# Sliding-window attention and a SwiGLU block: the tail tile of batches 2 and 3 in its own turn, attention paced closer, and most of block 5 moved to seven products

## The chip, the cores and the metric

The kernel runs on one core of a Trainium2 chip. The metric is device time of one execution in microseconds (us). Before the change the median of three runs is 332.56 us (332.44 to 333.28). One further execution was recorded by the hardware profiler; it took 333.68 us, and its first and last instruction are 331.9 us apart.

Engines are named as the profile names them: PE (matrix products; PEld is its weight load), DVE (vector), ACT (scalar), POOL (here only a queue that issues the loads) and SP (a queue that issues transposing DMAs and the stores).

## What is computed

The reference, cut to what matters (8 batches, 8 heads, 576 tokens, 64 values per head; 4608 tokens of 512 values; 1536 hidden columns):

```python
scores = q @ k.T / 8 - slope[h] * |i - j|          # only for 0 <= i - j < 128
x = (softmax(scores) @ v)                           # (4608, 512)
g, val = x @ w_gate, x @ w_val                      # (4608, 1536) each
out = (g * sigmoid(g) * val) @ w_out                # (4608, 512)
```

## The kernel before, in words

**Attention.** Two batches make a group `s` of nine tiles of 128 tokens: tiles p = 0 to 3 and 4 to 7 belong to one batch each, and p = 8, the tail tile, holds the last 64 tokens of both. That gives 36 units i = 9s + p, which are worked in order. `scores(i)` (L289) makes the products of a unit's keys with its own and the next tile's queries (`scores_128` or `scores_two` at the edges of a batch), takes the exponential on ACT and multiplies by the mask on DVE; `weighted(i)` (L406) multiplies by the values, and DVE divides by the sum (L431, L432). A group's tail tile needs two more sets of products: `scores_two` (keys of tiles 3 and 7, queries of the tail) and `tails()` (the tail with itself). In group 0 both are made at p = 8. In the later groups `tails()` is made together with the scores of p = 3 and `scores_two` together with those of p = 7.

**Where q and k come from.** POOL's queue loads each rank's q, k and v in order (`load`, `load_qk`, `load_v`); the q and k tiles have five buffers each (L143). From rank 11 on SP's queue transposes them by DMA (`transpose`, L247) into `kT` (12 slots) and `qT` (9 slots). `order` (L232) is the order of the transposes, `need` how many must be done before a unit, `due(rank)` (L241) the unit by which `ahead(i)` (L920) may send one: all that are due by unit i + AHEAD (4) and loaded are sent after unit i. In groups 1 to 3 the tail's q and k are loaded right behind rank 9s + 3 (L905) and transposed right behind the group's fourth tile, five ranks before their turn. The x tile of a unit is transposed by SP too (L451), and the stores share that queue; POOL's and SP's orders are fixed by hand from unit 7 on.

**The feed-forward part.** The 4608 rows of x are nine blocks of 512 tokens; block 8 holds the tails. For blocks 0 to 5 `gate_val(n, m)` makes one of twelve hidden columns of 128 from four products with w_gate and four with w_val, each 512 wide (L488): tanh on ACT and a `scalar_tensor_tensor` on DVE for the gate (L506, L507), a copy on ACT and a product on DVE for the value (L520, L521). Blocks 6 to 8 go by `gate_val_by_seven` (L714): a pair u of hidden columns is made as a 2 by 2 block product with seven instead of eight products, each four matmuls of width 256 (L726). These need sums of the weights, `gate_val_weight_sums(u)` (L696, four DVE instructions), and sums of x, `x_sums(n)` (L705, four), made beforehand. The output product of the block before, `strassen(n, t)` (L608, 2 times 7 parts of six matmuls, L636), is dealt out between these; its sums of h (`sums`, L598) are made when a block's later columns are done. In block 5 the columns after m = 7 use Silu in place of tanh, since attention, which needs the exponential, is over there: `attention_ends()` (L1073) sends what is left of it and issues the Silu once, which loads ACT's table.

**What sets the order.** `ffn()` (L806) yields a step after each piece: 1.0 after a gate or a value column, 0.75 after a part of `strassen`, 0.5 after a product of the seven. `everything()` (L1087) lets attention follow: after each step it calls `att_step()` until the number of attention steps reaches the target of L1116, 84 + (step - 57) * RATE / 34.5. A block of 34.5 steps (24 and 14 times 0.75) thus takes RATE = 54 attention steps, and a usual unit has nine. PE keeps this order to the end. DVE work that can wait is collected in `later` and issued one or two at a time. PSUM banks: scores, the weighted sums and two of the seven products' three tiles share four banks (`ps_a`); gate, value and the third have three (`ps_f`).

Of the kernel before, what the change touches and what calls it, by code (L numbers as in the profile page):

```python
# [32 lines left out]
PRE = 0  # L33
SEVEN_FROM = 6
SILU_AT = 7
SECOND = 5.5
RATE = 54.0
FIXED_FROM = 60
LATE = 13
VAL_COPIED_FROM = 2  # L40
# [16 lines left out]
def kernel(  # L57
# [175 lines left out]
    for s in range(NSUP):  # L233
        tails = [("k", 9 * s + 8), ("q", 9 * s + 8)]
        for half in (0, 4):
            order += [(name, 9 * s + half + r) for name, r in zip("kqqkqkqk", (0, 0, 1, 1, 2, 2, 3, 3))]
            order += tails if half == (0 if s else 4) else []
    need = [18 * s + n for s in range(NSUP)
            for n in ((3, 5, 7, 10, 13, 15, 17, 18, 18) if s else (3, 5, 7, 8, 11, 13, 15, 16, 18))]

    def due(rank):  # L241

        return rank - 5 if rank % 9 == 8 and rank > 8 else rank

# [44 lines left out]
    def scores(i):  # L289

        s, p = units[i]
        def tails():
            return scores_128(s, 8, 8, (s, "c"), msk, unit=i, more=True)

        def together(one, two):
            return [one[0] + two[0]] + one[1:] + two[1:]

        if p == 8:
            return [[]] * 3 + (together(scores_two(s, i), tails()) if s == 0 else [[]] * 2)
        if p in (3, 7):  # L300
            own = scores_128(s, p, p, (s, p), reg[:, :, 0:P], i < FIRST, i)
            return own if s == 0 else together(own, tails() if p == 3 else scores_two(s, i, True))
        ks = (9 * s + p) % NK
# [191 lines left out]
    acted = {}  # L495
    by_silu = set()

    def gate(n, m, pg, c0=0, c1=512):

        if (n, m) not in acted:  # L500
            acted[(n, m)] = [supool.tile([P, 512], FP16, name=i, tag=i) for i in ("tt", "uu")]
        tt, uu = (t_[:, c0:c1] for t_ in acted[(n, m)])
        if (n, m) in by_silu:
            nc.scalar.activation(tt, pg[:, c0:c1], AF.Silu)
            return
        nc.scalar.activation(tt, pg[:, c0:c1], AF.Tanh, scale=0.5)  # L506
        nc.vector.scalar_tensor_tensor(out=uu, in0=tt, scalar=one if (n, m) == PIN else 1.0,  # L507
                                       in1=pg[:, c0:c1], op0=ALU.add, op1=ALU.mult)

    def val(n, m, pv, c0=0, c1=512):  # L510

        if n not in hT:
            hT[n] = hpool.tile([P, NMB, 512], FP16, name="hT", tag="hT")
        if (n, m) in by_silu:
            nc.vector.scalar_tensor_tensor(out=hT[n][:, m, c0:c1], in0=acted[(n, m)][0][:, c0:c1], scalar=2.0,  # L515
                                           in1=pv[:, c0:c1], op0=ALU.mult, op1=ALU.mult)
            return
        if n >= VAL_COPIED_FROM:
            h = hT[n][:, m, :]
            nc.scalar.copy(h, pv)  # L520
            nc.vector.tensor_mul(h, acted[(n, m)][1], h)  # L521
            return
        nc.vector.tensor_mul(hT[n][:, m, c0:c1], acted[(n, m)][1][:, c0:c1], pv[:, c0:c1])
# [59 lines left out]

    one_more = []
    hsum = {}

    def four_sums(a11, a12, a21, a22, s2, s3, s4):

        return [lambda: nc.vector.tensor_sub(s3, a11, a21),
                lambda: nc.vector.tensor_add(a21, a21, a22),  # L590
                lambda: nc.vector.tensor_sub(s2, a21, a11),  # L591
                lambda: nc.vector.tensor_sub(s4, a12, s2)]

    def at_once(fs):
        for f in fs:
            f()

    def sums(n, c):  # L598
# [7 lines left out]
        return four_sums(a11, a12, a21, a22, s2, s3, s4)  # L606

    def strassen(n, t):  # L608
# [6 lines left out]
        end = n == NBLK - 1  # L615
        seeded = SEVEN_FROM <= n + 1 < NBLK
        factor = 1.0 if n >= SEVEN_FROM else 0.5
# [21 lines left out]
        def half_plus(dst, a, b):  # L639
            with tc.high_priority() if n + 1 < SEVEN_FROM else ExitStack():  # L640
                nc.vector.scalar_tensor_tensor(out=dst, in0=a, scalar=factor, in1=b,  # L641
                                               op0=ALU.mult, op1=ALU.add)

# [48 lines left out]
    spare += [halves(two_ex[:, 2 * n:2 * n + 2, :]) for n in range(4)]  # L692
    spare += [halves(msk[:, 0:4, :])]
    t_homes = [halves(kT[:, n]) for n in range(NK)] + [halves(qT[:, n]) for n in range(NQ)] + spare[6:9]

    def gate_val_weight_sums(u):  # L696

        cols = slice(2 * u * P, (2 * u + 2) * P)
        t1, t2, t3, t4 = tsum[u] = t_homes[4 * u:4 * u + 4]
        return [lambda: nc.vector.tensor_sub(t1, V1[:, :, cols], G1[:, :, cols]),  # L700
                lambda: nc.vector.tensor_sub(t3, V2[:, :, cols], V1[:, :, cols]),  # L701
                lambda: nc.vector.tensor_sub(t2, V2[:, :, cols], t1),
                lambda: nc.vector.tensor_sub(t4, G2[:, :, cols], t2)]

    def x_sums(n):  # L705

        a11, a12 = xT[n][:, 0:HK, 0:256], xT[n][:, HK:NKB, 0:256]
        a21, a22 = xT[n][:, 0:HK, 256:512], xT[n][:, HK:NKB, 256:512]
        s2, s3, s4 = xsum[n] = spare[3 * (n % 2):3 * (n % 2) + 3]
        return four_sums(a11, a12, a21, a22, s2, s3, s4)  # L710

    later = []

    def gate_val_by_seven(n):  # L714

        x = xT[n]
        A11, A12 = x[:, 0:HK, 0:256], x[:, HK:NKB, 0:256]
        S1, A22 = x[:, 0:HK, 256:512], x[:, HK:NKB, 256:512]
        S2, S3, S4 = xsum.pop(n)
        hT[n] = hpool.tile([P, NMB, 512], FP16, name="hT", tag="hT")  # L720
        live = {}
# [62 lines left out]
    def seven_steps():  # L784

        units = [(n, u) for n in range(SEVEN_FROM, NBLK) for u in range(NMB // 2)]
        of = {}
        for i, (n, u) in enumerate(units):
            if u == 0:
                of[n] = gate_val_by_seven(n)  # L790
# [15 lines left out]
    def ffn():  # L806

        for n in range(NBLK):
            if n > 1:
                parts = chain(strassen(n - 1, 0), strassen(n - 1, 1))  # L810
            if n == 1:
                begin(2, 2, 1)
                begin(3, 3, 1)
                for j in range(PRE):
                    for _ in project(0, j, ps_f, "po", 1):
                        yield 1.0
            if n == SEVEN_FROM:
                break
            due, given = 0, 0
            for m in range(NMB):  # L820
                for half, _ in enumerate(gate_val(n, m)):
# [17 lines left out]
                if n > 0 and m >= 9:  # L839
                    (at_once if n == 1 and m < 11 else later.extend)(sums(n, m - 9))  # L840
                if n + 1 == SEVEN_FROM:
                    if m == SILU_AT:
                        attention_ends()
                        by_silu.update((n, i) for i in range(m + 1, NMB))
                    if m in (SILU_AT + 1, SILU_AT + 2):
                        later.extend(gate_val_weight_sums(m - SILU_AT - 1))
                    if m == SILU_AT:
                        later.extend(x_sums(n + 1))
            if n > 1:
                assert next(parts, 0) == 0  # L850
        ends = [strassen(NBLK - 1, t) for t in range(2)]
        tail = ExitStack()
        for n, k, name, which in seven_steps():
            if k == 0 and n > SEVEN_FROM:
                assert next(parts, 0) == 0
                parts = chain(strassen(n - 1, 0), strassen(n - 1, 1))
            if n == SEVEN_FROM and k in (1, 3, 10, 17):
                later.extend(gate_val_weight_sums(2 + (k + 4) // 7))
            yield 0.5
            if k % 3 == 2 and k < 42:  # L860
                next(parts)
                yield 0.75
# [109 lines left out]
    def attention():  # L972
# [5 lines left out]
        for i in range(FIRST, last + 1):  # L978
# [175 lines left out]
```

## Time and profile before

| | |
|---|---|
| median of three runs | 332.56 us |
| profiled execution | 333.68 us, span 331.9 us, so 1.8 us lie outside the span |
| PE busy | 321.0 us (97%) |
| DVE busy | 261.6 us (79%) |
| ACT busy | 221.4 us (67%) |
| POOL, issuing loads | 111.3 us (34%) |
| mean granted TensorE clock | 0.997 |
| loads (POOL's queue), share of 16 engines' span | 79.2% |
| transposes and stores (SP's queue) | 33.9% |

"Busy" joins overlapping instructions. A matmul's record includes its way through the array, so that the means in the groups (363 ns for one of width 512) are longer than the distance between two starts; that distance is read from the chain of work, where consecutive matmuls of one kind are merged. The share of a DMA queue counts the time of its packets, which may overlap. A wait is put down to what came last.

The first products of blocks 2, 3, 4 and 5 start at 91.04, 127.03, 162.99 and 200.33 us; column 4 of block 5 starts at 212.56, column 8 at 225.06, block 6 at 235.22 us.

### The profile page before, as it was taken

How to read it: one execution, taken by the hardware profiler on the slowest of the kernel's cores; microseconds unless marked ns; L12 is line 12 of the kernel's file. 1: busy time of each engine (PE TensorE's matmuls, PEld its weight loads, DVE VectorE, ACT ScalarE, POOL GpSimd, SP SyncE). 2: the span in 40 equal slices, each digit the busy share in tenths (PEclk: the TensorE clock that was granted, in tenths of full speed). 3: DMA queues.
4: the chain of work that ended last, by engine and by line, in shares of the span. 5: the costliest groups of instructions: out<-in, count | busy, mean ns of one | idle time of the engine just before them, and what ended most of it. 6: DMA issues, size and time to landing. Idle time of an engine off the chain costs nothing. (4 is left out here: it accounts for less than half of the span.)

```text
span 331.9 us, 7661 instructions
## 1 busy us (share of the span) xinstructions
PE 321.0 (97%) x2911; PEld 215.3 (65%) x2911; DVE 261.6 (79%) x638; ACT 221.4 (67%) x438; POOL 111.3 (34%) x138
## 2 busy tenths in 40 slices
PE   8999999999799999999999999999999999999994
PEld 4665465444356665656655655565788888888883
DVE  4678879999597689887998799997854976765783
ACT  4976777365586678777677768753577766777650
POOL 8967777396572535545335100000000000000000
PEclk9999999999999999999999999999999999999998
DMA  9999999999999999999999993113100101001014
GB/s 152 170 181 176 173 178 169 123 121 171 154 150 197 142 163 155 189 136 175 157 144 187 139 182 81 46 28 85 65 32 34 64 2 63 34 35 64 2 63 129
DMA packets 167654, 39.09 MB, mean 118 GB/s; under 512 B 155456, under 2 KB 163264, under 8 KB 167616
## 3 DMA queue, kind: packets, MB, share of 16 engines
q0 software_dynamic: 118880, 18.62, 79.2%
q1 hardware_dynamic: 48048, 19.35, 33.9%
q10 hardware_dynamic: 688, 0.62, 0.6%
q8 instruction: 23, 0.38, 0.5%
q14 instruction: 15, 0.12, 0.1%
HBM read 37.91 MB, written 9.44 MB: 143 GB/s over the span
## 5 line engine op out<-in xcount | busy, mean ns | idle before, releaser
L488 PE MATMUL pv<-xT,wv_sb 128*128 128x512 f16 (+2 forms) x312 | 76.6, 363 | 0.3 <-DVE uu L507 0.2
L488 PE MATMUL pg<-xT,wg_sb 128*128 128x512 f16 (+2 forms) x324 | 76.5, 355 | 0.4 <-DVE hT L515 0.3
L506 ACT ACTIVATE tt<-pg 128x512 f16<-128x512 f32 x68 | 41.7, 614 | 26.5 <-PE pg L488 25.1
L333 ACT ACTIVATE ex<-ps 128x512 f16<-128x512 f32 x96 | 51.0, 612 | 7.6 <-PE ps L327 7.6
L507 DVE SCALAR_TENSOR_TENSOR uu<-tt,pg 128x512 f16<-128x512 f16 x67 | 45.7, 683 | 8.3 <-ACT tt L506 7.9
L197 POOL DMA_DIRECT2D kn<-in_k_dram x39 | 33.3, 854 | 44.0 <-DMA kT<-kn 31.9
L488 PEld LDWEIGHTS <-wg_sb 128*128 128x128 f16 x324 | 29.6, 98 | 26.2 <-issue 2.6
L636 PEld LDWEIGHTS <-hT 128*128 128x128 f16 x384 | 37.0, 98 | 10.0 <-issue 1.0
L488 PEld LDWEIGHTS <-wv_sb 128*128 128x128 f16 x312 | 27.4, 98 | 22.9 <-issue 2.3
L520 ACT CAST hT<-pv 128x512 f16<-128x512 f32 x44 | 26.0, 592 | 19.4 <-PE pv L488 19.3
L197 POOL DMA_DIRECT2D qn<-in_q_dram x39 | 33.3, 860 | 15.4 <-DMA qn<-in_q_dram 8.5
L191 POOL DMA_DIRECT2D va<-in_v_dram x40 | 34.2, 861 | 10.6 <-DMA va<-in_v_dram 4.1
L339 DVE TENSOR_TENSOR ex<-ex,m_reg 128x1024 f16<-128x1024 f16 x42 | 28.9, 689 | 7.7 <-ACT ex L333 7.5
L636 PEld LDWEIGHTS <-S 128*128 128x128 f16 x288 | 27.6, 98 | 7.9 <-issue 1.1
L432 DVE TENSOR_TENSOR x<-av,rec 128x256 f16<-128x256 f32 x72 | 29.0, 421 | 0.6
L636 PE MATMUL po<-T,hT 128*128 128x256 f16 x192 | 26.1, 273 | 0.0
L636 PE MATMUL po<-T,S 128*128 128x256 f16 x192 | 25.9, 273 | 0.0
L521 DVE TENSOR_TENSOR hT<-uu,hT 128x512 f16<-128x512 f16 x44 | 18.5, 421 | 4.0 <-ACT hT L520 3.8
L780 DVE TENSOR_TENSOR hT<-s,v 128x512 f16<-128x512 f16 x18 | 7.6, 424 | 17.7 <-ACT s L779 17.7
L428 PEld LDWEIGHTS <-ex 128*128 128x128 f16 x384 | 17.6, 98 | 5.7 <-issue 1.2
L428 PE MATMUL av<-va,ex 128*128 128x65 f16 x384 | 19.2, 193 | 0.7 <-ACT ex L333 0.3
L327 PE MATMUL ps<-qT,kT 64*128 64x256 f16 x192 | 15.3, 271 | 2.8 <-DMA qT<-qn 2.0
(138 smaller groups left out, 556.4 us busy)
## 6 DMA issues: line engine op xcount, KB each, us to landing
out_dram<-osb SPq DMA_DIRECT2D x32, 256.0 KB, 2.3
va<-in_v_dram POOLq DMA_DIRECT2D x32, 128.0 KB, 10.3
qn<-in_q_dram POOLq DMA_DIRECT2D x31, 128.0 KB, 9.7
kn<-in_k_dram POOLq DMA_DIRECT2D x31, 128.0 KB, 8.6
wg_sb<-in_moe_w_gate_dram POOLq DMA_DIRECT2D x6, 256.0 KB, 7.6
wo_sb<-in_moe_w_out_dram POOLq DMA_DIRECT2D x3, 512.0 KB, 8.2
wv_sb<-in_moe_w_val_dram POOLq DMA_DIRECT2D x5, 256.0 KB, 8.1
kn<-in_k_dram POOLq DMA_DIRECT2D x8, 64.0 KB, 9.3
```

The lines of the kernel that those rows point to most:

```text
L191: nc.gpsimd.dma_start(va[rank][p0:p1, :, 0:D], src)
L197: nc.gpsimd.dma_start(t_[p0:p1], src)
L333: nc.scalar.activation(e[:, o:o + 2, :], banks[q4][par], AF.Exp, scale=scale)
L339: nc.vector.tensor_mul(e[:, o, :], e[:, o, :], reg[:, o, :])
L428: nc.tensor.matmul(av[:, j, :], w, val, start=(n == 0), stop=(n == len(todo) - 1))
L432: nc.vector.tensor_mul(x[:, 4 * half:4 * half + 4, :], av[:, :, 0:D], rec.broadcast_to([P, 4, D]))
L488: close.after = nc.tensor.matmul(ps[:, c0:c1], w[:, kb, ms], xT[n][:, kb, c0:c1], start=(kb == 0 and c0 == 0), stop=(kb == NKB - 1 and c1 ...
L506: nc.scalar.activation(tt, pg[:, c0:c1], AF.Tanh, scale=0.5)
L507: nc.vector.scalar_tensor_tensor(out=uu, in0=tt, scalar=one if (n, m) == PIN else 1.0, in1=pg[:, c0:c1], op0=ALU.add, op1=ALU.mult)
L520: nc.scalar.copy(h, pv)
L521: nc.vector.tensor_mul(h, acted[(n, m)][1], h)
L636: nc.tensor.matmul(dst, a[:, m, cols], b[:, m, :], start=(start and m == 0), stop=(m == HM - 1), skip_group_check=True)
```

## The change

`SEVEN_FROM` goes from 6 to 5 with `UNIT_FROM = 2`: block 5 makes its first four columns (m = 0 to 3) as before and the other eight as the pairs u = 2 to 5 by seven products. The Silu columns of the old scheme go. Attention is paced by RATE 59 and ended after block 5's column 3. `turns` orders the pairs 2, 3, 4, 5, 0, 1: the weight sums of pairs 2 and 3 are issued at attention units 29 and 30, the sums of block 5's x at unit 31, those of pairs 4, 5, 0 and 1 during block 5's products; they get other homes in freed slots of `kT` and `qT` and in the masks. The tail of group 1 (batches 2 and 3) is loaded, transposed and scored in its turn as rank 17: `tails()` at p = 8, `scores_two` still at p = 7. From unit 14 on transposes are sent one unit earlier. `strassen(4, 1)` is made in the seeded form. The copy of the value columns becomes a multiplication by 1.0 (0.5 in block 5).

```diff
-SEVEN_FROM = 6
-SILU_AT = 7
+SEVEN_FROM = 5
+UNIT_FROM = 2
-RATE = 54.0
+RATE = 59.0
+EARLIER_FROM = 14
...
-            order += tails if half == (0 if s else 4) else []
+            order += tails if half == (0 if s > 1 else 4) else []
...
-        return rank - 5 if rank % 9 == 8 and rank > 8 else rank
+        return rank - 5 if rank % 9 == 8 and rank > 17 else rank
...
-            return scores_128(s, 8, 8, (s, "c"), msk, unit=i, more=True)
+            return scores_128(s, 8, 8, (s, "c"), msk, unit=i, more=s != 1)
...
-            return [[]] * 3 + (together(scores_two(s, i), tails()) if s == 0 else [[]] * 2)
+            return (tails() if s == 1 else [[]] * 3) + (together(scores_two(s, i), tails()) if s == 0 else [])
...
-            return own if s == 0 else together(own, tails() if p == 3 else scores_two(s, i, True))
+            if s < (2 if p == 3 else 1):
+                return own
+            return together(own, tails() if p == 3 else scores_two(s, i, True))
...
-            nc.scalar.copy(h, pv)
+            nc.scalar.mul(h, pv, 0.5 if n == SEVEN_FROM else 1.0)
...
-        seeded = SEVEN_FROM <= n + 1 < NBLK
+        seeded = SEVEN_FROM <= n + 1 < NBLK and (n >= SEVEN_FROM or t > 0 or UNIT_FROM == 0)
...
+            for m in range(2 * UNIT_FROM if n == SEVEN_FROM else NMB):
...
+        at_once(later)
+        later.clear()
+        attention_ends()
...
-            if n == SEVEN_FROM and k in (1, 3, 10, 17):
-                later.extend(gate_val_weight_sums(2 + (k + 4) // 7))
+            if n == SEVEN_FROM and k in (16, 20, 26, 30):
+                later.extend(gate_val_weight_sums(turns[{16: 2, 20: 3, 26: 4, 30: 5}[k]]))
...
-            if k % 3 == 2 and k < 42:
-                next(parts)
+            if k % 3 == (1 if n == SEVEN_FROM else 2) and k < 42 and next(parts, 1) is None:
                 yield 0.75
...
-            for _ in range(2 if len(later) > 4 or k < 7 else 1):
+            for _ in range(1 if n == SEVEN_FROM and k < 21 else 2 if len(later) > 4 or k < 7 else 1):
                 if later:
-                    later.pop(0)()
+                    with tc.issue_after(added[0].ins) if n == SEVEN_FROM else ExitStack():
+                        later.pop(0)()
...
-            if rank % 9 == 8:
+            if rank % 9 == 8 and rank > 17:
                 load_v(rank)
             else:
                 load(rank)
-            if rank % 9 == 3:
+            if rank % 9 == 3 and rank > 18:
                 load_qk(rank + 5)
...
-        while by_dma and due(order[by_dma[0]][1]) <= min(i + AHEAD, loaded - 1):
+        reach = i + AHEAD + (i >= EARLIER_FROM)
+        while by_dma and due(order[by_dma[0]][1]) <= min(reach, loaded - 1):
...
+            if i in (29, 30):
+                later.extend(gate_val_weight_sums(turns[i - 29]))
+            if i == 31:
+                later.extend(x_sums(SEVEN_FROM))
             loads_to(i + 7)
             ahead(i)
```

More of the change, by code (lines that the diff above doesn't have):

```diff
@@ L236 @@
             order += [(name, 9 * s + half + r) for name, r in zip("kqqkqkqk", (0, 0, 1, 1, 2, 2, 3, 3))]
-            order += tails if half == (0 if s else 4) else []
+            order += tails if half == (0 if s > 1 else 4) else []
     need = [18 * s + n for s in range(NSUP)
-            for n in ((3, 5, 7, 10, 13, 15, 17, 18, 18) if s else (3, 5, 7, 8, 11, 13, 15, 16, 18))]
+            for n in ((3, 5, 7, 10, 13, 15, 17, 18, 18) if s > 1 else (3, 5, 7, 8, 11, 13, 15, 18 if s else 16, 18))]
     def due(rank):
-        return rank - 5 if rank % 9 == 8 and rank > 8 else rank
+        return rank - 5 if rank % 9 == 8 and rank > 17 else rank
     last_qk = []
@@ L495 @@
     acted = {}
-    by_silu = set()
     def gate(n, m, pg, c0=0, c1=512):
@@ L502, in gate @@
         tt, uu = (t_[:, c0:c1] for t_ in acted[(n, m)])
-        if (n, m) in by_silu:
-            nc.scalar.activation(tt, pg[:, c0:c1], AF.Silu)
-            return
         nc.scalar.activation(tt, pg[:, c0:c1], AF.Tanh, scale=0.5)
@@ L513, in val @@
             hT[n] = hpool.tile([P, NMB, 512], FP16, name="hT", tag="hT")
[L514 to L517, printed above, removed]
         if n >= VAL_COPIED_FROM:
             h = hT[n][:, m, :]
-            nc.scalar.copy(h, pv)
+            nc.scalar.mul(h, pv, 0.5 if n == SEVEN_FROM else 1.0)
             nc.vector.tensor_mul(h, acted[(n, m)][1], h)
@@ L584, with four_sums @@
     one_more = []
+    added = []
     hsum = {}
[L587 to L592, printed above, removed]
+    def four_sums(a11, a12, a21, a22, s2, s3, s4, s1=None, eng=nc.vector):
+        s1 = a21 if s1 is None else s1
+        return [lambda: eng.tensor_sub(s3, a11, a21),
+                lambda: eng.tensor_add(s1, a21, a22),
+                lambda: eng.tensor_sub(s2, s1, a11),
+                lambda: eng.tensor_sub(s4, a12, s2)]
     def at_once(fs):
@@ L596, in at_once, with sums @@
             f()
-    def sums(n, c):
+    def sums(n, c, eng=nc.vector):
         if n not in hsum:
@@ L605, in sums @@
         s2, s3, s4 = (t_[:, lo, :] for t_ in hsum[n])
-        return four_sums(a11, a12, a21, a22, s2, s3, s4)
+        return four_sums(a11, a12, a21, a22, s2, s3, s4, eng=eng)
     def strassen(n, t):
@@ L639, in half_plus @@
         def half_plus(dst, a, b):
-            with tc.high_priority() if n + 1 < SEVEN_FROM else ExitStack():
-                nc.vector.scalar_tensor_tensor(out=dst, in0=a, scalar=factor, in1=b,
-                                               op0=ALU.mult, op1=ALU.add)
+            with tc.high_priority() if n <= SEVEN_FROM else ExitStack():
+                added[:] = [nc.vector.scalar_tensor_tensor(out=dst, in0=a, scalar=factor, in1=b,
+                                                           op0=ALU.mult, op1=ALU.add)]
         product(X, A11, B11, True)
@@ L692 @@
     spare += [halves(two_ex[:, 2 * n:2 * n + 2, :]) for n in range(4)]
-    spare += [halves(msk[:, 0:4, :])]
-    t_homes = [halves(kT[:, n]) for n in range(NK)] + [halves(qT[:, n]) for n in range(NQ)] + spare[6:9]
+    spare += [halves(msk[:, 4 * n:4 * n + 4, :]) for n in range(2)]
+    early_homes = [halves(t_[:, n]) for t_, n in ((kT, 0), (kT, 1), (kT, 2), (kT, 3), (qT, 0), (kT, 4),
+                                                  (qT, 1), (kT, 5), (qT, 2), (qT, 3), (kT, 7), (qT, 4),
+                                                  (kT, 8), (qT, 5), (kT, 9), (qT, 6))]
+    late_homes = [halves(t_[:, n]) for t_, n in ((kT, 6), (kT, 10), (kT, 11), (qT, 7), (qT, 8))] + spare[3:10]
+    turns = [(UNIT_FROM + n) % (NMB // 2) for n in range(NMB // 2)]
+    t_homes = dict(zip(turns, (early_homes[0:4], early_homes[4:8], early_homes[12:16],
+                               late_homes[0:4], late_homes[4:8], late_homes[8:12])))
+    x_homes = {SEVEN_FROM: early_homes[8:11] + early_homes[11:12]}
+    for n in range(SEVEN_FROM + 1, NBLK):
+        x_homes[n] = early_homes[8:11] if (n - SEVEN_FROM) % 2 == 0 else spare[0:3]
     def gate_val_weight_sums(u):
         cols = slice(2 * u * P, (2 * u + 2) * P)
-        t1, t2, t3, t4 = tsum[u] = t_homes[4 * u:4 * u + 4]
+        t1, t2, t3, t4 = tsum[u] = t_homes[u]
         return [lambda: nc.vector.tensor_sub(t1, V1[:, :, cols], G1[:, :, cols]),
@@ L708, in x_sums @@
         a21, a22 = xT[n][:, 0:HK, 256:512], xT[n][:, HK:NKB, 256:512]
-        s2, s3, s4 = xsum[n] = spare[3 * (n % 2):3 * (n % 2) + 3]
-        return four_sums(a11, a12, a21, a22, s2, s3, s4)
+        s2, s3, s4 = x_homes[n][0:3]
+        s1 = x_homes[n][3] if n == SEVEN_FROM else a21
+        xsum[n] = s1, s2, s3, s4
+        return four_sums(a11, a12, a21, a22, s2, s3, s4, s1, nc.vector)
     later = []
@@ L717, in gate_val_by_seven @@
         A11, A12 = x[:, 0:HK, 0:256], x[:, HK:NKB, 0:256]
-        S1, A22 = x[:, 0:HK, 256:512], x[:, HK:NKB, 256:512]
-        S2, S3, S4 = xsum.pop(n)
-        hT[n] = hpool.tile([P, NMB, 512], FP16, name="hT", tag="hT")
+        A22 = x[:, HK:NKB, 256:512]
+        S1, S2, S3, S4 = xsum.pop(n)
+        if n not in hT:
+            hT[n] = hpool.tile([P, NMB, 512], FP16, name="hT", tag="hT")
         live = {}
@@ L784, in seven_steps @@
     def seven_steps():
-        units = [(n, u) for n in range(SEVEN_FROM, NBLK) for u in range(NMB // 2)]
+        units = [(n, u) for n in range(SEVEN_FROM, NBLK)
+                 for u in range(UNIT_FROM if n == SEVEN_FROM else 0, NMB // 2)]
         of = {}
         for i, (n, u) in enumerate(units):
-            if u == 0:
+            if n not in of:
                 of[n] = gate_val_by_seven(n)
@@ L816, in ffn @@
                         yield 1.0
-            if n == SEVEN_FROM:
+            due, given = 0, 0
+            if n == SEVEN_FROM and not UNIT_FROM:
                 break
-            due, given = 0, 0
-            for m in range(NMB):
+            for m in range(2 * UNIT_FROM if n == SEVEN_FROM else NMB):
                 for half, _ in enumerate(gate_val(n, m)):
@@ L840, in ffn @@
                     (at_once if n == 1 and m < 11 else later.extend)(sums(n, m - 9))
[L841 to L848, printed above, removed]
+            if n == SEVEN_FROM:
+                break
             if n > 1:
                 assert next(parts, 0) == 0
+        at_once(later)
+        later.clear()
+        attention_ends()
         ends = [strassen(NBLK - 1, t) for t in range(2)]
```

## The prediction

> **What bounds the kernel now.** I read the stretches first: busy time of the engines per block. The columns are the stretch in us, its length, then busy us (instructions) of PE, PEld, DVE, ACT and POOL, the clock, the DMA share and GB/s. The first three lines are blocks 2 to 4, then block 5 up to column 4, its columns 4 to 7, and a full block of seven products.
>
> ```profile
> 91.04:127.03 35.99, 35.99 (x327) 21.64 (x326) 29.25 (x74) 26.57 (x54) 18.03 (x22) 1.00 1.85 162
> 127.03:162.99 35.96, 35.96 (x334) 21.74 (x332) 31.28 (x81) 27.12 (x55) 17.16 (x22) 1.00 1.79 160
> 162.99:200.33 37.34, 36.90 (x334) 22.09 (x332) 33.02 (x87) 27.23 (x55) 9.43 (x12) 1.00 1.67 164
> 200.33:212.56 12.23, 12.23 (x120) 7.45 (x119) 12.23 (x34) 9.65 (x21) 0.00 (x0) 1.00 0.26 74
> 212.56:225.06 12.50, 12.07 (x120) 7.75 (x118) 11.00 (x30) 8.21 (x15) 0.00 (x0) 1.00 0.13 22
> 262.70:290.20 27.50, 27.46 (x253) 24.44 (x251) 20.05 (x46) 19.32 (x39) 0.00 (x0) 1.00 0.10 39
> ```
>
> PE fills nearly every stretch at full clock, so a removed matmul is time, as long as nothing else falls behind. DVE is next: 81 to 88% in blocks 2 to 4, and wholly busy for the 12 us from 200.33, which PE stood without a gap. ACT has a quarter free.
>
> The chain of work that ended last gives PE's pace, and it holds to the end (start, us, what):
>
> ```profile
> 231.94 0.86 PE pv L488 x4
> 232.80 0.86 PE pg L488 x4
> 233.67 0.69 PE po L636 x6
> 234.35 0.86 PE pv L488 x4
> 235.22 0.44 PE gX L726 x4
> ```
>
> Four matmuls of width 512 take 0.864 us, four of width 256 take 0.437, six 0.656. Last, the waits and the order of time around PE's longest gap:
>
> ```profile
> POOL kn L197 <- DMA kT<-kn: 31.9, 8, 6.6
> PE ps L327 <- DMA qT<-qn: 2.0, 2, 1.6
> ```
>
> ```profile
> 63.75 1.48 POOL L197 DMA_DIRECT2D kn<-in_k_dram  x2 [6.63 <-DMA kT<-kn]
> 65.22 1.37 POOL L197 DMA_DIRECT2D qn<-in_q_dram  x2
> ...
> 77.29 1.33 SPq L253 DMA_TRANSPOSE qT<-qn  x1
> ...
> 79.96 0.38 PE L394 MATMUL psc<-qT,kT 64*128 64x128 f16 x4 [0.29 <-PE psc L394]
> ...
> 84.90 0.39 PE L327 MATMUL ps<-qT,kT 64*128 64x256 f16 x4 [1.58 <-DMA qT<-qn]
> ```
>
> The four half loads at 63.75 are the tail of group 1, issued ahead of rank 13; the transpose at 77.29 is q of rank 14, and at 84.90 unit 13's scores have waited 1.58 us for it. All other recorded waits of PE behind 91 us sum to 1.6 us (gaps of 0.6 at 192.3, 0.6 at 214.6, 0.4 at 229.6).
>
> **Part 1, the seven products: -1.6 us.** A pair of plain columns is 16 matmuls of width 512: 4 x 0.864 = 3.46 us. A pair by seven is 28 of width 256: 7 x 0.437 = 3.06. Four pairs save 1.6 us of PE, all on the path. Beside it come on DVE: four more sums of x (4 x 0.42), and per pair 2 x 0.69 and 2 x 0.42 (rows of L763, L771, L764, L780) = 2.2 us, where two tanh columns have 2 x (0.68 + 0.42) = 2.2 and two Silu columns 2 x 0.69 = 1.4; in all 1.7 + 2 x 0.8 = 3.3 us more, hidden while DVE has room. ACT gets 2.9 us per pair (five rows of 0.57 to 0.60) for 2.4, of its free quarter. The value copy as a multiplication is a row of 598 ns (L559) for 592: nothing. The seeded `strassen(4, 1)` swaps a copy for a scaling and one bank for another of the three gate banks: nothing either way by rows of 358 and 385, 423 and 420 ns.
>
> The Trainium skill (TensorE: Matmul & The Clock Gate, Back-to-back issue gap) speaks against this part: it gives a sustained 81 ns per matmul of width 128 and 131 ns for 512 in streams of load and product. By an estimate between these, 98 ns for 256, 28 would take 2.7 us and 16 only 2.1, and four pairs would lose 2.6 us. The chain shows 216 and 109 ns, so I don't take it; the same section's single-gap formula fits.
>
> **Part 2, the tail in its turn: -1.7 us.** Without the four half loads (2.9 us of POOL's queue) and the tail's two transposes (SP's queue, 1.3 us each) in front, rank 13 to 16 come 2 to 3 us earlier; q of rank 14 waited only for its load, so 1.58 us of wait go, and with them the 0.29 at 79.96, where tails and own scores asked for four banks at once. Against it 0.2 us: products of 64 rows at p = 8 by themselves pay the two switches (about 0.1 us each) seen before and after every set of scores. What is late next: q of ranks 15 and 16, needed about 1 us after they land; they move up equally. The tail's own k and q now land behind rank 16's, needed at unit 16 (102.08). SP is idle there for 4 us (89.4 to 93.9), so two transposes of 1.2 us fit, about 1 us ahead of need. Bounds: 0 (the wait moves to the next units) and -1.9; I take -1.7, since POOL's queue itself is shorter.
>
> **Part 3, the pace.** Counting the yields of `attention()`, 289 steps become 281 (2 fewer at p = 3 of group 1, 2 at each later p = 8). The target reaches the end at step 57 + 205 x 34.5 / 54 = 188.0 before and 57 + 197 x 34.5 / 59 = 172.2 after. Block 5 starts at 163.5, its column 3 ends at 175.25, so little is left for `attention_ends()`. A block's own PE work is 24 x 0.864 + 14 x 0.656 = 29.9 us, a unit 1.0 (block 3: 36.0 less 29.9, six units). Units go from 6 to 6.6 per block, so from one in 6.0 us to one in 5.6. PE's sum does not change by that.
>
> Transposes: a q lands 7 to 9 us after it is sent (median 8.1), as long as loads run. The unit of lead from `EARLIER_FROM` gives 5.6 us back, and frees POOL's buffers that much earlier, for which it waited 31.9 us. What stands behind a transpose that waits for its load on SP are x tiles and stores; x of group 1's second batch is sent from 93.9 on and block 3 starts at 127, so these have 10 us or more. Taken at 0, bounds 0 and +4.8 (second rival).
>
> DVE: from 91 to the start of the seven it has 116.8 us now up to column 8; less four columns (4.4), parts of `strassen` (1.3) and sums done there now (3.8), plus the new ones (5.1), 112 us in 123, 92% for 87%. In block 5's seven products it has 8.9 (four pairs), 6.7 (16 weight sums), 1.7 (x of block 6), 1.7 (`half_plus`), 1.7 (sums of h), together 20.7, of which 1.7 can wait into block 6: 19.0 us beside PE's 28 x 0.437 + 9 x 0.656 = 18.1. I take +0.5; bounds 0 (the 12.2 us at 100% cost nothing) and +2.2.
>
> Start of the seven: their PSUM banks are those of the last weighted sums, and ACT loads its table there. Now, with the banks long free, the first product at 235.22 waits for nothing:
>
> ```profile
> 214.50 1.28 ACT L1079 ACT_TABLE_LOAD   x1
> 215.94 0.21 ACT L1079 ACTIVATE turn<-two_ex 128x1 f16<-128x1 f16 x1 [0.16 <-DVE two_ex L368]
> ```
>
> Bounds 0 and +1.9 (1.28 and one copy of 0.6 in front of PE); I take +0.5, as the part of `strassen` covers 0.66. The Trainium skill (ScalarE: Activation LUTs, What ACT_TABLE_LOAD costs) adds a drain of 1.38 us, by which the upper bound would be 3.3. Here the next activation follows 0.16 us after the load's end, so I leave it out. The three small waits behind 91 us (1.6) I leave in the sum: their like will come, elsewhere.
>
> **Sum:** -1.6 - 1.7 + 0.5 + 0.5 = **-2.3 us**. The profiled execution would be 331.4 for 333.68. It lies 1.1 above the median of the runs; from the median, 332.56 - 2.3 = **330.3 us**.
>
> **Rivals.**
> *The wait moves (chance 0.10):* q of ranks 15 to 17, about 1 us ahead of need, take the wait over, since PE comes 2 us earlier. Then part 2 gives nothing: 331.9.
> *Loads can't go faster (0.22), slower:* the transposes take 2.4 us from 196 us on, when loads have ended, and 8 beside them, so they share engines. From 124 to 160 us POOL issued 18 loads' worth, waiting not for buffers but for its own landings: 2.0 us each, 6.0 per unit of three; the new pace asks for 5.6. If the last ones land no earlier, q for unit 33, there at about 199.8 (sent 195.33, 4.5 us), meets scores that would start at 204.8 - 1.7 - 19 x 0.43 = 195.0: PE loses 4.8 us. Sum -3.3 + 4.8 + 0.3 = +1.8: 334.4. It decides when the deficit passes the 2.3 us gained. The skill (DMA: Bandwidth & Descriptors, Issuing engines are not separate DMA queues) states that sharing. Against it: 31.9 us in which POOL waited for buffers, most of them outside that stretch.
> *DVE bounds block 5 (0.10):* the upper bounds +2.2 and +1.0 in place of the 1.0: -3.3 + 3.2 = -0.1: 332.5.
> *Attention isn't over at column 3 (0.03):* the rest goes in one piece in front of the seven; a unit's chain of scores, exponential, mask and sums, some 4 us, is then bare: 333.5.
>
> **Numbers.** The forecast has 0.55: with the small waits gone and no new ones, -3.3 - 1.6 = 327.7; with 1 us more of new ones, 331.3. Range 327.7 to 333.8: it leaves out most of the second rival (0.15) and little below. A measurement can tell 0.3%, 1.0 us, from no change. Faster: the forecast, half of the first rival: 0.60. Same: the other half and the third: 0.16. Slower: 0.24.
>
> **What would show it.** Part 1: 64 fewer matmuls at L488, 112 more of width 256 in the seven products, and block 5's second part in 18 to 19 us. Part 2: no wait of L327 for qT at unit 13. Part 3: last transposes of q sent at about 188, attention over before the first product of seven; a sum of `ps <- qT` waits above 3 us would show the second rival, PE waiting for DVE's v or sums in block 5 the third.

## The result and the profile after

The changed kernel takes 335.84 us (median of 11 runs, 335.16 to 338.37); the kernel before, on the same chips, 333.49 (11 runs, 332.44 to 334.85). The ratio is 1.0069, 95% interval 1.0049 to 1.0090: 2.3 us slower, where 2.3 us faster was forecast. The profiled execution took 335.84 us with a span of 334.1 (before 333.68 and 331.9).

First the stretches of the kernel after, with the same columns as in the prediction: blocks 2, 3 and 4, then block 5's four plain columns, then its eight columns by seven products.

```profile
88.40:126.00 37.60, 37.60 (x366) 22.64 (x365) 32.23 (x81) 29.32 (x60) 21.21 (x26) 1.00 1.88 163
126.00:165.67 39.67, 37.34 (x358) 22.66 (x356) 33.20 (x86) 28.16 (x56) 16.34 (x21) 1.00 1.72 167
165.67:206.41 40.74, 37.08 (x350) 22.30 (x349) 33.94 (x89) 29.96 (x60) 8.14 (x10) 1.00 1.28 123
206.41:218.35 11.94, 11.73 (x103) 7.32 (x102) 10.35 (x29) 7.43 (x14) 0.00 (x0) 1.00 0.55 122
218.35:236.96 18.61, 18.57 (x169) 16.23 (x166) 17.28 (x46) 12.76 (x26) 0.00 (x0) 1.00 0.12 44
```

Block 2 begins 2.6 us earlier than before (91.04), block 5 6.1 us later (200.33). A block is longer for two reasons. It holds more attention (366, 358 and 350 matmuls for 327, 334 and 334), which costs nothing in sum, since block 5 holds less. And PE stands still: blocks 3 and 4 take 39.67 and 40.74 us, of which PE works 37.34 and 37.08. So 6.0 us are idle, where blocks 3 and 4 of before have 0.4.

What PE waits for (us in total, times, longest); these rows lie behind 88 us:

```profile
PE ps L330 <- DMA qT<-qn: 3.2, 2, 2.5
PE ps L330 <- issue: 1.7, 1, 1.7
...
PE ps L330 <- DVE osb L638: 1.1, 1, 1.1
```

The timeline has the rows (start, duration, what, idle time before it and its releaser):

```profile
132.42 0.61 PE L330 MATMUL ps<-qT,kT 64*128 64x256 f16 x8 [1.66 <-issue]
...
144.50 0.61 PE L330 MATMUL ps<-qT,kT 64*128 64x256 f16 x8 [0.67 <-DMA qT<-qn]
...
172.42 0.38 PE L330 MATMUL ps<-qT,kT 64*128 64x256 f16 x3 [1.14 <-DVE osb L638]
...
191.62 0.61 PE L330 MATMUL ps<-qT,kT 64*128 64x256 f16 x8 [2.52 <-DMA qT<-qn]
```

These are scores of units 22, 24, 29 and 32. The first is labelled "issue", but q's transpose for rank 23 landed at 132.33, 0.09 us before: it is the same wait as the second and the fourth. By the distance of two starts, less the usual distance (0.216 us at width 512), the three cost 1.82, 0.84 and 2.68 us, together **5.3 us for q**; the one for DVE costs 1.3.

What led to the last one is seen on SP's queue:

```profile
180.26 1.06 SPq L538 DMA_DIRECT2D out_dram<-osb  x2
181.56 1.32 SPq L254 DMA_TRANSPOSE qT<-qn  x1
```

The load of q for rank 33, issued by POOL at 168.68, landed at 181.54; the transpose went out at once and landed at 191.48, 9.9 us later. Here no queue was late; the transfers were. On POOL the waits have changed their kind:

```profile
POOL kn L198 <- DMA va<-in_v_dram: 8.5, 4, 3.3
POOL qn L198 <- DMA qn<-in_q_dram: 7.2, 6, 2.4
POOL kn L198 <- DMA kT<-kn: 6.9, 1, 6.9
```

The wait for buffers (kT<-kn) fell from 31.9 us to 6.9, as the earlier transposes should make it; the waits for its own landings rose instead. POOL issued the last load at 178.2 instead of 183.4 us, and yet it landed at 193.96 instead of 195.06: 5 us sooner issued, 1 us sooner there. From 124 to 200 us the transfers moved 162 GB/s before and 157 after.

**The balance.** All stops of PE of over 0.3 us between 60 and 260 us, by the same measure: before 0.45 (79.5), 1.74 (83.1, unit 13's q), 0.61, 0.59 and 0.44, in sum 3.8 us. After: 0.41 (79.3), the 5.3 for q, the 1.3 for DVE, and 0.30 and 0.34 at 238 and 243, in sum 7.7. That is +3.9. Part 1 took 64 matmuls of 0.216 us off and put 112 of 0.109 on: -1.6. Together +2.3; the span grew by 2.2.

### The profile page after: what moved, and what is told of

It reads as the page before. It is cut to its first block, busy times and chain, and to the rows that moved or that the text cites. A ratio compares the mean times of both kernels' runs of the same rounds, so it can differ in the third digit from the quotient of the medians.

```text
span 334.1 us, 7776 instructions
## 1 busy us (share of the span) xinstructions
PE 319.9 (96%) x2959; PEld 219.7 (66%) x2959; DVE 264.7 (79%) x646; ACT 225.9 (68%) x446; POOL 111.2 (33%) x138
## 4 chain that ended last, share of the span: by engine, by line
PE 46%; DMA 30%; DVE 11%; issue 5%; POOL 4%; ACT 2%; DVEq 0%; POOLq 0%
DMA qn<-in_q_dram 20%; PE po L633 11%; PE gX L735 10%; DMA va<-in_v_dram 7%; PE gY L735 5%; PE pg L491 4%; PE pv L491 4%; DMA qT<-qn 3%; PE gZ L735 2%; DVE uu L506 2%; PE p L633 2%; PE av L431 2%; POOL qn L198 2%; POOL kn L198 1%; PE ps L330 1%
## 5 line engine op out<-in xcount | busy, mean ns | idle before, releaser
L491 PE MATMUL pv<-xT,wv_sb 128*128 128x512 f16 (+2 forms) x280 | 68.3, 361 | 0.4 <-DVE uu L506 0.2
L491 PE MATMUL pg<-xT,wg_sb 128*128 128x512 f16 (+3 forms) x292 | 68.3, 353 | 0.1
L505 ACT ACTIVATE tt<-pg 128x512 f16<-128x512 f32 x64 | 38.7, 606 | 28.0 <-PE pg L491 26.6
L506 DVE SCALAR_TENSOR_TENSOR uu<-tt,pg 128x512 f16<-128x512 f16 x63 | 42.9, 680 | 8.0 <-ACT tt L505 7.6
L491 PEld LDWEIGHTS <-wg_sb 128*128 128x128 f16 x292 | 26.0, 98 | 22.5 <-issue 2.2
L491 PEld LDWEIGHTS <-wv_sb 128*128 128x128 f16 x280 | 24.7, 98 | 22.2 <-issue 3.1
L515 ACT ACTIVATE hT<-pv 128x512 f16<-128x512 f32 x40 | 24.2, 605 | 13.5 <-PE pv L491 13.5
L789 DVE TENSOR_TENSOR hT<-s,v 128x512 f16<-128x512 f16 x22 | 9.3, 422 | 16.7 <-ACT s L788 16.7
L330 PE MATMUL ps<-qT,kT 64*128 64x256 f16 x192 | 15.8, 271 | 6.8 <-DMA qT<-qn 3.2
L516 DVE TENSOR_TENSOR hT<-uu,hT 128x512 f16<-128x512 f16 x40 | 16.8, 419 | 3.3 <-ACT hT L515 2.7
## 6 DMA issues: line engine op xcount, KB each, us to landing
kn<-in_k_dram POOLq DMA_DIRECT2D x8, 64.0 KB, 12.6
```

The source lines that it names most:

```text
L491: close.after = nc.tensor.matmul(ps[:, c0:c1], w[:, kb, ms], xT[n][:, kb, c0:c1], start=(kb == 0 and c0 == 0), stop=(kb == NKB - 1 and c1 ...
L515: nc.scalar.mul(h, pv, 0.5 if n == SEVEN_FROM else 1.0)
```

## The experiments

The expectations name theories by letters. Theory A, formed from the profile above: loads and transposes share one limit, the new pace asks for more than it gives, and that costs the 5.3 us. Where the limit sits (the DMA engines or the memory behind them) no run here shows. The rivals on which the runs turned: B, it is DVE that PE waits for, directly or through what DVE frees; D, the phase, that is where the attention steps fall against the parts of `strassen`; G, the loads are limited by themselves, and the transposes don't share that limit. What these and the others expect of a run is said in each expectation. "Padded" means that attention steps which the change drops are kept as empty ones. The diffs show the lines that matter; "..." stands for others.

**The tail alone, and the pace alone.** The first takes the tail's lines of the diff into the kernel before (RATE 54, no column of block 5 by seven; the empty steps at p = 8 stay), the second these two values and the line of `ahead` that uses the new one:

```diff
-RATE = 54.0
+RATE = 59.0
+EARLIER_FROM = 14
...
```

> The kernel before with the tail of batches 2 and 3 in its turn and nothing else (the empty steps at later tail tiles stay, so the pace is that of before but for two steps). Theory A (loads and transposes together are at their limit, and a faster pace of attention is repaid in PE waits for q): the wait of 1.6 us at unit 13 goes and no new one comes, since the pace leaves 1 to 4 us of lead; 1.5 to 2 us faster than before. Theory B (DVE's extra work took the gain): the same 1.5 to 2 us. Theory C (the tail in its turn itself makes later q land late, by pushing the loads of ranks 17 and up together): 0 to 2 us slower, with waits of L327 or its successor for q at units 16 to 24.

> The kernel before with RATE 59 and the transposes one unit earlier from unit 14, nothing else: plain columns in block 5, the tail as before. PE's work is that of before. Theory A: the wait at unit 13 stays, and 3 to 6 us of new waits for q appear from 124 us on; 2 to 5 us slower than before; the last load lands at 193 to 196 us as in both kernels so far. Theory B: DVE has no more work than before, only closer together; at most 1 us slower.

The tail alone: 334.11 us against 334.24, ratio 0.9995 (0.9975 to 1.0015). The pace alone: 336.04, ratio 1.0077 (1.0049 to 1.0105). So the pace alone slows the kernel as much as the whole change does, which theory B (at most 1 us) did not allow, and the tail's gain is missing when it is alone. But theory A's 3 to 6 us of waits for q behind 124 us are missing too:

```profile
PE ps L328 <- DMA qT<-qn: 3.3, 2, 2.0
...
187.79 0.61 PE L328 MATMUL ps<-qT,kT 64*128 64x256 f16 x8 [1.29 <-DMA qT<-qn]
```

By distance of starts this one is 1.45 us and unit 13's 2.2 (1.74 before). All stops over 0.3 us between 60 and 260 us sum to 4.8 us for 3.8, while the span is 1.7 us longer (333.6 for 331.9); where the rest went was not found. What PE waited for in the tail kernel:

```profile
PE ps L329 <- DMA qT<-qn: 1.2, 1, 1.2
PE pv L490 <- DVE uu L509: 1.1, 2, 0.9
PE po L638 <- ACT u2s L664: 1.0, 4, 0.3
```

Two things ate it; the waits for q at units 16 to 24 that theory C expected are not there. Unit 13's wait is still 1.2 us in this run, though POOL and SP have the same order of DMAs up to there as in the changed kernel: the loads were issued at the same times but landed later in this run (k of rank 13: issued at 63.7 in both, landed at 69.74 for 68.27), so that q's transpose went out at 74.65 instead of 72.98 us and landed at 82.80 instead of 81.05. And two attention steps fewer, at p = 3 of group 1, shift all that follows, so that at 101.72, 138.65, 175.15 and 211.80, once per block, two parts of `strassen` have only one value column's four products between them and the second waits for ACT to empty a bank (0.4 us each by distance of starts, 1.7 in all); waits for DVE at 217.57, 226.80 and 231.20 cost 2.0 (their like cost 1.0 before).

**The changed kernel without v's loads from rank 18 on** (attention then works on old values):

```diff
         va[rank] = va_all[rank % NV]
+        if rank >= 18:
+            return
```

> The changed kernel without the v loads from rank 18 on (those units use the values that lie in the buffers, so the output is another), about a third less to load from 85 us on. PE, DVE and ACT do the same work. Theory A: the waits for q at 130, 143 and 189 us (5.3 us) go, about 5 us faster than the changed kernel and some 3 us faster than before (0.99). Theory B: the waits stay or turn into waits for DVE; within 1 us of the changed kernel (1.007 of before).

331.34 us, ratio 0.9926 (0.9902 to 0.9950). With a third of the loads gone the waits for q go, and the one for DVE stays ("PE ps L332 <- DVE osb L640: 1.1, 1, 1.1"). So DVE's 1.1 us are its own, and q's waits are not made by DVE: B holds for the small one only. From 124 to 166 us, while loads still ran, q's transposes took 4.4 us in the median for 8.1 in the changed kernel, and the transfers moved 164 GB/s for 166: with fewer loads the transposes went faster and the total stayed.

**The changed kernel without the transposes of q and k from rank 18 on** (attention then works on old q and k):

```diff
         t_ = (natk if name == "k" else natq).pop(rank)
+        if rank >= 18:
+            return
```

> The changed kernel without the transposing DMAs of q and k from rank 18 on (those units take what lies in the slots, so the output is another); all loads stay. Theory A (loads and transposes share one limit): with two of three transposes gone the loads from rank 18 on land about 1 us apart instead of 1.9 and the last one by 150 to 175 us instead of 194; the waits for q go; 4 to 6 us faster than the changed kernel. Rival G (the loads are bound by POOL's own queue, whatever else runs): the last load lands at 190 us or later.

331.09 us, ratio 0.9906 (0.9870 to 0.9942). Waits for q can't occur here from rank 18 on, so the time alone decides nothing; the loads do. The longest wait of PE behind 88 us, then the last loads on POOL:

```profile
PE ps L332 <- DVE osb L640: 1.2, 1, 1.2
```

```profile
161.20 0.90 POOL L192 DMA_DIRECT2D va<-in_v_dram  x1 [20.68 <-PE av L433]
...
163.81 2.28 POOL L192 DMA_DIRECT2D va<-in_v_dram  x3
```

This is the run that decides between A and G. All loads are still there, yet they are so far ahead that POOL waits 20.7 us for PE to free a v buffer; the last lands at 170.2, 4.9 us after its issue, where the changed kernel's landed at 194.0, 15.8 us after. Part of that lead has another cause: without its transpose a q or k buffer is free as soon as its load has landed. The better measure is therefore the time of one load from its issue; from 124 to 200 us, in the changed kernel and then in this one (number, size, median us to landing):

```profile
qn<-in_q_dram POOLq DMA_DIRECT2D x8, 128.0 KB, 12.6
...
qn<-in_q_dram POOLq DMA_DIRECT2D x6, 128.0 KB, 7.9
```

From 85 to 124 us, before PE held POOL up, it was 7.2 us for 12.5, and the transfers moved 169 GB/s for 161. The transposes slow the loads down: G falls, and with the run without v's loads, where the loads slowed the transposes, it is shown that the two share a limit. How the pace meets this limit is seen in the runs below.

**More buffers:** `nat` 5 to 6, and `op` 7 to 6 to make room.

> The changed kernel with six buffers for the loaded q and k tiles (and six instead of seven for the stores, for room). Theory A (memory side at its limit in total): POOL's 6.9 us wait at 57 us shrinks, loads begin up to 5 us sooner and the last one lands up to 5 us sooner; the waits for q fall from 5.3 to 0 to 2 us, so 3 to 5 us faster than the changed kernel (0.993 to 0.998 of before). If the wait at 57 us stays as it is, nothing changes (1.007). Rival F (each load's delay is set by the count of buffers all along, a closed loop): the loads run faster everywhere, with the same start, and the gain is the same; the landings between 100 and 190 us then lie less than 1.9 us apart.

335.99 us, ratio 1.0051 (1.0024 to 1.0077). Nothing was gained, and POOL's wait of 6.8 us for a buffer of k near 60 us stayed, the case for which the expectation has 1.007. Of q's waits two stayed (1.73 and 2.34 us by distance of starts, 4.1 for 5.3). One buffer more doesn't help; the last load lands at 193.1. Since the extra buffer took no wait away, the run says little beyond that.

**Half of it:** only columns 8 to 11 of block 5 by seven products, at the old rate, transposes still earlier (with the weight sums of pairs 2 and 3 in block 6, the sums of block 6's x later, and `strassen(4, 1)` as before).

```diff
-UNIT_FROM = 2
+UNIT_FROM = 4
-RATE = 59.0
+RATE = 54.0
...
```

> The changed kernel with UNIT_FROM 4 (only pairs 4 and 5 of block 5 by seven) and RATE 54, so that attention may end behind column 7 of block 5, at about the pace of before; strassen(4, 1) unseeded as before, weight sums of pairs 2 and 3 in block 6. Theory A: the old pace has no wait for q beyond 1 us, so the tail's 1.7 us and half of the seven's 1.6 us show: 1.5 to 2.5 us faster than before (0.993 to 0.996). Theory B: the sums of x and weights still come on DVE in block 5; no more than 1 us faster than before.

334.13 us, ratio 1.0009 (0.9993 to 1.0026), where A expected 1.5 to 2.5 us less than before. No waits for q, as A has it, but a new place:

```profile
236.28 0.39 PE L633 MATMUL p<-wo_sb,hT 128*128 128x256 f16 x2 [0.71 <-DVE hT L773]
...
240.16 0.39 PE L633 MATMUL po<-T,hT 128*128 128x256 f16 x2 [1.74 <-DVE hT L587]
```

At the start of block 6 DVE had the sums of w_gate and w_val, of x and of h to make at once, and PE stood for h, 2.8 us by distance of starts; waits for ACT at 100.37 and 211.59, of the kind that the tail alone had, cost 1.4. The first is like the third rival of the prediction, but in block 6 and in a kernel in which I put those sums too close, and not in the change itself.

**The tail, padded:** the tail alone, with the two dropped steps at p = 3 of group 1 kept as empty ones (the number at p = 8 was kept in both).

```diff
-                return own
+                return own + ([[]] * 2 if s == 1 else [])
```

> The tail of batches 2 and 3 in its turn as in the first experiment, and two empty attention steps each put back at p = 3 and p = 8 of that group, so that every later piece of attention stands beside the same piece of the feed-forward part as before the change. Theory D (the first experiment gained at unit 13 and gave it back because the shifted pace put two parts of strassen behind one another, where PE waits for ACT's copy, four times about 0.4 us): these four waits are absent; 1 to 2 us faster than before. Theory E (the wait at unit 13 just stays, since q of rank 14 lands no sooner relative to PE): within 0.5 us of before, the wait of L327's successor for q at unit 13 over 1 us in the profile.

331.02 us, ratio 0.9909 (0.9881 to 0.9937), 3.0 us faster than before. Unit 13's wait is 0.3, and no wait for ACT's copy is left. The same work as in the tail alone, two empty steps, and 3 us between them. By distance of starts the stops over 0.3 us fell from 5.5 to 1.5 us: 0.9 of it is unit 13's q, which landed 1.2 us sooner here, the other 3 are ACT's four waits and DVE's. D holds for these, and E falls. That the tail in its turn brings nothing, as its run alone let one think, falls too.

**Half of it, padded,** with the weight sums of pairs 1, 2 and 3 moved into block 6 (1, 8 and 15 products into it) and the sums of x sooner than in the run before that. Of the edit against the changed kernel, the lines of the weight sums:

```diff
-            if n == SEVEN_FROM and k in (16, 20, 26, 30):
-                later.extend(gate_val_weight_sums(turns[{16: 2, 20: 3, 26: 4, 30: 5}[k]]))
+            if (n, k) in (at := {(SEVEN_FROM, 30): 2, (SEVEN_FROM + 1, 1): 3, (SEVEN_FROM + 1, 8): 4, (SEVEN_FROM + 1, 15): 5}):
+                later.extend(gate_val_weight_sums(turns[at[n, k]]))
...
```

> The changed kernel with pairs 4 and 5 of block 5 by seven, RATE 54 and the empty steps of the fifth experiment, and the weight sums of pairs 1, 2 and 3 only in block 6, so that DVE is not crowded where the fourth experiment showed PE waiting 2.4 us for it (sums of h and a product of h at the start of block 6). Theory A with D: no wait for q above 1 us, the waits at the start of block 6 under 1 us; 1.5 to 3 us faster than before (0.991 to 0.996). If DVE is crowded all the same: the waits at 235 to 239 us stay above 2 us, and the time is that of before.

**329.58 us, ratio 0.9865 (0.9837 to 0.9893): 4.3 us faster than before and the fastest of all that ran.** The stretches of its blocks 2, 3 and 4:

```profile
88.26:124.68 36.42, 36.42 (x334) 21.78 (x333) 29.84 (x75) 27.45 (x56) 19.47 (x24) 1.00 1.85 166
124.68:160.64 35.96, 35.96 (x333) 21.74 (x332) 31.27 (x81) 27.14 (x55) 15.00 (x19) 1.00 1.73 164
160.64:197.47 36.83, 36.83 (x333) 22.05 (x332) 33.18 (x88) 27.26 (x55) 10.13 (x12) 1.00 1.65 165
```

PE's busy time equals the stretch in all three, at the GB/s of the changed kernel's blocks 2 and 3 (163 and 167): what the limit delivers, this pace does not exceed. Since the empty steps and the places of the sums changed together, the run doesn't say what each gave against the half unpadded. On the same chip it is 1.4 us faster than the padded tail, which has neither the two pairs by seven (0.8 by count) nor the earlier sending.

**The changed kernel, padded, at RATE 59; and the padded half without `EARLIER_FROM`.**

> The changed kernel (all eight columns by seven products, RATE 59) with the empty attention steps of the padded kernels: two after p = 3 and two after p = 8 of group 1, two after p = 8 of the later groups, so 289 attention steps again. The target reaches the end at step 57 + 205 x 34.5 / 59 = 176.9 instead of 172.2, still some 11 steps earlier than at RATE 54. Theory A (the transposes of q and their loads share one limit, and the pace asks for more than it): the waits of L330 for q between 126 and 200 us stay, 3 to 6 us of PE, and the time is 334 to 336, 1.000 to 1.007 of before. Rival D (what hurt the changed kernel was mostly where the steps fell against the products of h and w_out, as with the tail alone): the waits go as they did in the padded tail kernel, and the time is 329 to 331, 0.987 to 0.992 of before.

> The padded kernel with four columns of block 5 by seven products at RATE 54, but with no transpose sent a unit earlier (EARLIER_FROM = 99). Theory A: at this pace the loads keep up, and the earlier sending buys nothing that PE sees: 329.1 to 330.3, 0.985 to 0.990 of before, waits of L330 for q at most 1 us. Rival: the earlier sending is what took the q waits away there: then waits of 1 to 3 us for q come back at units 13 to 30, and the time is 330.5 to 332.5.

The first: 331.96 us, ratio 0.9955 (0.9934 to 0.9976), between the two expectations, and both missed. Its waits for q and its blocks 3 and 4:

```profile
PE ps L330 <- DMA qT<-qn: 0.9, 1, 0.9
```

```profile
125.23:163.59 38.36, 38.18 (x366) 22.74 (x365) 33.92 (x90) 28.38 (x57) 16.42 (x20) 1.00 1.74 164
163.59:201.21 37.62, 36.55 (x323) 21.66 (x320) 33.83 (x89) 28.07 (x56) 8.69 (x11) 1.00 1.44 147
```

The last load lands at 193.0, 1 us sooner than in the changed kernel. But 289 steps at RATE 59 end at step 176.9 instead of 172.2, some 5 us later, and that is nearly all that was lacking: unit 32's scores come at 190.25, q landed at 189.8 (in the changed kernel PE was free at 188.9 and q landed at 191.5). The deficit is a matter of few us against a nearly fixed date, not of a share. The waits for q over 0.3 us behind 88 us, by distance of starts, in the kernels with every transfer (the step in brackets is the one at which the target reaches the end):

| | RATE 54 | RATE 59 |
|---|---|---|
| all 289 steps | 0.6 before, 0 tail padded, 0 half padded, 0.8 half padded without `EARLIER_FROM` (188.0) | 1.5 pace alone, 1.0 change padded (176.9) |
| eight dropped, 281 steps | 0 half (182.9) | 5.3 change, 4.1 with six buffers (172.2) |

The tail alone, with 287 steps at RATE 54, has none. So neither RATE nor the dropped steps alone made the 5.3 us; the two together did. RATE moved the end by 11.1 steps and the dropped steps by 4.7, yet the larger part of the wait came with the latter. The same change with eight empty steps is 1.1% faster. Since the empty steps move the phase too, what part of the 1.1% is phase stays open.

The second: 330.15 us (329.38 to 331.35), ratio 0.9906 (0.9883 to 0.9929), against 0.9865 (0.9837 to 0.9893) with `EARLIER_FROM`. Waits for q are 0.7 us ("PE ps L330 <- DMA qT<-qn: 0.7, 1, 0.7"), under the 1 us of theory A. The median lies inside A's range, the ratio just outside it and the intervals overlap: whether the earlier sending is worth up to 0.4% there is open.

## Why the prediction was wrong

- **Part 1, -1.6: right.** The matmuls at `gate_val` fell by 64 and those of the seven rose by 112, and the eight columns took 18.6 us, as foretold (18 to 19). PE works 18.57 us of them, with DVE busy 17.28: the DVE that was to bind block 5 (third rival) did not. One reading in this part is off without effect: the columns that went by Silu had one row on ACT and not two (L504, four rows of 598 ns), so ACT got 2.9 us for 1.2 in two of the four pairs; it is busy for 12.76 of the 18.61 us.
- **Part 2, -1.7: right in the profile of the changed kernel, but no fixed gain.** Unit 13's scores no longer wait and start at 81.63 instead of 84.90. The tail kernels show what the step left out: the gain varies with the landing of one q (0, 0.3 or 1.2 us of wait in the changed kernel, the padded tail and the tail alone, whose orders of DMAs are the same up to there), and the steps that vanish at p = 3 and p = 8 shift everything behind them. Alone, the tail gained nothing, with the two dropped at p = 3; padded, it gave 3.0 us, of which unit 13 is 1.3 and small waits that also went are 1.0. That the term came out right here is in part luck: unit 13's wait was 1.74 by distance of starts and went whole, while the 0.29 at 79.96 went and a wait for DVE of the same size came at 79.72.
- **Part 3, transposes, "taken at 0, bounds 0 and +4.8": the step that failed.** It cost 5.3 us. The reason given was that the unit of lead frees POOL's buffers earlier, and that 31.9 us of waiting for buffers lay outside the stretch of the second rival. The buffers did come free, and POOL did issue 5 us sooner, but that reserve was no bandwidth: the last load landed at 191 to 197 us in every kernel with all transfers, whatever the pace (195.06 before, 193.96 after). I read a queue's waiting as room in the transfers behind it. The eight dropped steps were counted in the pace (172.2) and priced at nothing as well; without them the waits at RATE 59 are 1.0 to 1.5 us.
- **The second rival was the mechanism,** with the sharing that it named, now shown by the runs without transposes and without v. Its total, +1.8, came near the +2.3 measured partly by luck: it saw one wait of 4.8 us at unit 33, and there were three, at units 22, 24 and 32. It had a chance of 0.22, though its own row (2.0 us per load where the pace asked for less) was the one row of the profile that measured the limit.
- **Small terms.** DVE +0.5: 1.3, and not in block 5 but at unit 29, where scores waited for a bank behind DVE's sum of an output tile. Start of the seven +0.5: PE is idle 0.2 us in the four columns before and nothing stands at the first product (218.35); ACT loaded its table at 206.41, twelve us ahead of it, since the last exponential was done by then. Old small waits, "their like will come": 1.64 went (0.61, 0.59, 0.44), and 0.64 came (0.30, 0.34).

With 5.3 in place of 0 and 1.3 + 0.2 in place of 1.0 the sum is -3.3 + 5.3 + 1.5 - 1.0 = +2.5, for +2.3 measured.

## What to carry to other kernels

Before a consumer is paced faster, find the date by which the last transfer can land at the rate that the trace shows, and count the pace back from it; a queue that waits for buffers has no room to give if the transfers it has issued already take longer than they do alone (q's loads 11.2 us before the change, 7.9 without the transposes). When steps are dropped from an interleaved order, keep their places empty first and see what the removal alone is worth, since the shift of everything behind it can cost more. Two parts of a change that each cost little can cost much together (here the dropped steps and the rate); the smaller size is then the better buy: the padded tail gave 3.0 us and half the columns at the old rate with it 4.3, where the whole lost 2.3.

## What the runs showed of the hardware

- Loads, transposing DMAs and stores together moved 157 to 162 GB/s from 124 to 200 us in all ten kernels with every transfer, and no order or pace among them raised it. A q load took 7.9 us in the median without the transposes and 12.6 with them, a transpose of q 4.4 us without v's loads and 8.1 with them (124 to 166 us).
- The same order of DMAs on both queues lands up to 1.8 us apart from one profiled run to the other (q for unit 13 at 81.05, 81.62 and 82.80 us in the changed kernel, the padded tail and the tail alone, whose POOL queues issued the loads before it within 0.1 us of each other), enough to make or unmake a wait where the data was planned 1 us ahead of need.
- A wait for a DMA can be labelled "issue" in the profile: at 132.42 only the landing at 132.33 tells it.
